# Pooled attention into soft mixture-of-experts slots, on one core: a first load in two parts, fewer and larger whole-row stores, fewer weight loads

## The chip, the core and the metric

The kernel runs on one core of a Trainium2 chip. The metric is the time of one execution on the device in microseconds (us). Engines are named as in the profile: PE is TensorE (its weight loads are PEld), DVE VectorE, ACT ScalarE, POOL GpSimd, SP SyncE. Transfers between memory and the on-chip buffers run on 16 DMA engines. Two queues feed them here: POOL issues the software transfers (q0 in the profile), which can turn float32 into bfloat16 on the way, and SP issues the hardware transfers (q1). SPq and POOLq mean the sequencers of these engines.

## The reference

```python
def attn(q, k, v):                       # each [8, 8, 576, 64] float32
    k_p = k.reshape(B, H, 72, 8, D).mean(axis=3)      # keys pooled by 8
    v_p = v.reshape(B, H, 72, 8, D).mean(axis=3)
    scores = (1 / sqrt(D)) * (q @ k_p.transpose(0, 1, 3, 2))
    return softmax(scores) @ v_p
def moe(x, phi, w1, w2):                 # x [4608, 512], phi [512, 32]
    logits = x @ phi                     # 8 experts x 4 slots
    slot_input = softmax(logits, over tokens).T @ x
    for e in range(8):                   # w1[e] [512, 1024], w2[e] [1024, 512]
        slot_out[e] = relu(slot_input[e] @ w1[e]) @ w2[e]
    return softmax(logits, over slots) @ slot_out      # [4608, 512] float32
```

The inputs are 28.3 MB of q, k and v and 33.6 MB of w1 and w2, all float32; the output is 9.4 MB.

## The kernel before, in words

**Attention.** The batch is worked off in four pairs (`NP`), two batch rows each. For each pair, `prepare_kq` pools the keys by matrix products with `pmat` (`pool_stage`), turns them and turns the queries; `prepare_v` does the same for the values and folds phi in by `iphi`. `score_unit` makes the scores and their exponentials, `u_tile` the weighted sums, `combine` (with `dispatch` and `turn`) adds the pair to the slot sums `G` and writes the transposed exponentials to `cT`.

**Loads.** Four buffers `big[:, 0..3]` hold k, q and v of the pairs in turn. `load` puts one of them in the POOL queue as a software transfer of 128 partitions by 4608 elements. The hooks `after_k`, `after_q` and `after_v` are called where a buffer has been read for the last time, and issue the next loads: first those of the next pair, then w1 (`load_w1`, into `w1_sb`), then w2 (`load_w2`, into the buffers that are free by then: `big`, `qTa`, `xsa`). The last expert and half of the one before come in eight pieces (`PIECES` times two halves of the columns, L446). POOL works in its written order. A software transfer signals one of eight semaphores in turn, so its issue can also wait for the landing of the transfer eight places ahead of it.

The very first load is different: the first 4 x 8 x 64 keys of each partition (128 rows of 8 KB, 1 MB) come by the SP queue as float32 into `kf` (L121), and DVE and ACT turn them to bfloat16 (L154, L155). The rest of these keys is the first transfer of the POOL queue (L122).

**Experts.** After the last pair, `hidden(0)` and `hidden(1)` multiply the slot inputs by w1 (four experts each), `turn_hidden` transposes, and `second_layer` multiplies by w2, expert by expert, into `so_ps`. The engines PE, ACT, DVE and SP work in the written order from here. The last expert's columns are done in two halves, so that `begin(0)` and `tiles` can scale and store the left half of the first ten output tiles while w2 for the right half is still coming.

**Output.** The 36 output tiles of 128 tokens by 512 columns are gathered in groups. A group of `rows` tiles covers 128 x `rows` consecutive tokens; partition p holds `rows` consecutive output rows, so a store of the whole group writes `rows` x 2 KB in one run for each partition. `tokens(n)` picks the columns of `cT` for a tile with a step of rows/2. The first four groups (2, 2, 2 and 4 tiles) are stored in halves of the columns. The others are stored whole, as soon as the group's last tile has been scaled by DVE or ACT (`put`, alternating), by one SP transfer each (`store`, L545).

Of the kernel before, what the change touches and what calls it, by code (L numbers as in the profile page):

```python
# [18 lines left out]
def kernel(  # L19
# [10 lines left out]
    nc = tc.nc  # L30
# [11 lines left out]
    NP = B // 2  # L42
# [11 lines left out]


    GROUPS, base = [], 0
    for rows in (2, 2, 2, 4, 4, 6, 10, 6):
        GROUPS.append((rows, base))
        base += 128 * rows
    TILES = [(g, r) for g, (rows, _) in enumerate(GROUPS) for r in range(rows)]  # L60
# [8 lines left out]
    big = persist.tile([128, 4, KQ], BF)  # L69
# [15 lines left out]
    def pair_of(src, pair):  # L85
        return src[2 * pair:2 * pair + 2].rearrange("b h (i t) d -> (b h i) (t d)", t=NT)
# [10 lines left out]
    def load(src, pair):  # L97
        nonlocal loaded
        loaded += 1
        t = big[:, loaded % 4]  # L100
        nc.gpsimd.dma_start(out=t, in_=pair_of(src, pair))
        return t.rearrange("p (t d) -> p t d", d=D)

    def load_w1(e, n, parts=((0, 128),)):
        for p0, p1 in parts:
            nc.gpsimd.dma_start(out=w1_sb[p0:p1, e:e + n].rearrange("p e j f -> p e (j f)"),
                                in_=moe_w1[e:e + n].rearrange("e (p j) f -> p e (j f)", j=DJ)[p0:p1])
# [3 lines left out]
    def load_w2(home, e, n, j0=0, j1=FJ):  # L111
        for i in range(n):
            for j in range(j0, j1):
                w2_at[e + i, j] = home[:, i, j * DM:(j + 1) * DM]
        nc.gpsimd.dma_start(out=home[:, 0:n, j0 * DM:j1 * DM],
                            in_=moe_w2[e:e + n].rearrange("e (p j) d -> p e j d", j=FJ)[:, :, j0:j1].rearrange("p e j d -> p e (j d)"))


    CUT = 4 * POOL * D
    kf = exf[:, 0:CUT]  # L120
    nc.sync.dma_start(out=kf, in_=pair_of(k, 0)[:, 0:CUT])  # L121
    nc.gpsimd.dma_start(out=big[:, 0, CUT:KQ], in_=pair_of(k, 0)[:, CUT:KQ])  # L122
    q_sb, k_sb, v_sb = {}, {}, {}
    k_sb[0] = big[:, 0].rearrange("p (t d) -> p t d", d=D)
# [37 lines left out]
    with tc.tile_pool(name="tmp", bufs=1) as tmp:  # L162
# [8 lines left out]
        for r in range(2):  # L171
            rows = slice(r * D, (r + 1) * D)
            nc.vector.tensor_copy(out=iphi[rows, :, 0:D],
                                  in_=ident[rows, rows].rearrange("p d -> p () d").to_broadcast([D, H, D]))
# [25 lines left out]
    def after_k(p):  # L200
        if p + 1 < NP:
            q_sb[p + 1] = load(q, p + 1)
        if p == 1:
            load_w1(0, 1, ((0, 112), (112, 120), (120, 128)))
        if p == NP - 1:
            load_w2(big[:, 0:2], 0, 2)

    def after_q(p):
        if p + 1 < NP:
            v_sb[p + 1] = load(v, p + 1)  # L210
        if p == 1:
            load_w1(1, 1)
        if p == 2:
            load_w1(2, 2)
            load_w1(4, 2)
            load_w1(6, 2)

    def after_v(p):
        if p + 2 < NP:
            k_sb[p + 2] = load(k, p + 2)  # L220
        if p == NP - 1:
            load_w2(big[:, 2:4], 2, 2)

    PARTS = ((0, 4), (4, NR))

# [23 lines left out]
    def prepare_kq(pair):  # L249

        means = kvpool.tile([128, NR, 2, D], BF, name="kmeans")
        yield from pool_stage(k_sb[pair], means, lambda: after_k(pair))
        kp[pair] = kvpool.tile([128, BH, SP], BF, name="kp", bufs=2)
        yield from turn_stage(means, kp[pair])
        for n, t0 in enumerate(range(0, NU, 6)):
            ps = ps_m.tile([128, 6, BH, NI], BF, name="q_ps", tag="m")
            for t in range(6):
                tt = 2 * (t0 + t)
                nc.tensor.transpose(out=ps[:, t].rearrange("p n i -> p (n i)"),  # L259
                                    in_=q_sb[pair][:, tt:tt + 2, :].rearrange("p t d -> p (t d)"), identity=ident)  # L260
            dst = qT[pair][:, :, t0:t0 + 6, :].rearrange("p n t i -> p t n i")
            if n % 3 == 1:
                nc.scalar.copy(out=dst, in_=ps)  # L263
            else:
                nc.vector.tensor_copy(out=dst, in_=ps)  # L265
            if n == NU // 6 - 1:
                after_q(pair)
            yield

    def prepare_v(pair):  # L270

        means = kvpool.tile([128, NR, 1, D], BF, name="vmeans")
        yield from pool_stage(v_sb[pair], means, lambda: after_v(pair))
        vpar = kvpool.tile([D, BH, SP], BF, name="vpar")
        yield from turn_stage(means, vpar)
        for b in range(2):
            for qd in range(2):
                ps = ps_m.tile([SP, HQ, XW], FP, name="v_ps", tag="m")
                for hh in range(HQ):
                    h = qd * HQ + hh  # L280
                    nc.tensor.matmul(out=ps[:, hh], lhsT=vpar[:, b * H + h], rhs=iphi[0:D, h], start=True, stop=True)
                nc.scalar.copy(out=vp[(2 * pair + b) % 5][:, qd * HQ:(qd + 1) * HQ, 0:XW], in_=ps)
                yield
# [158 lines left out]
    for half, cols in enumerate(halves):  # L442
        for e, j0, j1 in PIECES:
# [3 lines left out]
                                in_=moe_w2[e].rearrange("(p j) d -> p j d", j=FJ)[:, j0:j1, cols])  # L447
# [188 lines left out]
```

## Time and profile before

| | |
|---|---|
| median of 3 runs | 176.18 us (175.78 to 176.47) |
| the profiled execution, its own time | 175.6 us |
| its span, first to last instruction | 173.8 us |
| PE, DVE, ACT busy | 74%, 52%, 48% of the span |
| software queue q0 | 7072 packets, 30.48 MB written, 86.4% of 16 engines |
| hardware queue q1 | 3456 packets, 10.49 MB, 15.4% |
| HBM read, written | 61.93 MB, 9.44 MB |

The profile covers one execution. Its span is cut into 40 slices of 4.35 us, for which the page gives each engine's busy share in tenths and the DMA engines' share and rate. The rate counts the bytes as they are written: a load that turns float32 into bfloat16 reads twice the bytes it is counted with. So about 216 GB/s of such loads and about 435 GB/s of float32 loads or stores are the same load on the read side or the write side of the DMA engines.

### The profile page before, as it was taken

Reading aid. Unit: us, or ns where it says so; the run is one execution under the profiler, and the core shown is the slowest. Engines: PE = TensorE matmul, PEld = TensorE weight load, DVE = VectorE, ACT = ScalarE, POOL = GpSimd, SP = SyncE. Lnnn points to the kernel's source line nnn. Section 1 sums busy time; section 2 is a strip of 40 time slices with the busy share of each in tenths; the row PEclk is TensorE's granted clock in tenths of the full one; section 3 lists DMA queues with packets and bytes.
Section 4 is the critical chain, followed back from the end, with each engine's and each line's share of the span. In section 5 each row is a group of like instructions: output and inputs, shape, how many; then the busy total and the mean of one; then the engine's idle time right before and its main releaser. Section 6 shows DMA issues by size and latency. Waiting matters only on the chain.

```text
span 173.8 us, 3094 instructions
## 1 busy us (share of the span) xinstructions
PE 129.4 (74%) x1239; PEld 76.9 (44%) x1240; DVE 90.9 (52%) x251; ACT 83.0 (48%) x155; POOL 20.3 (12%) x38
## 2 busy tenths in 40 slices
PE   5205889999999998979998897889973096798000
PEld 2003555766677665756765455534451032332000
DVE  4403242487777879758798668614260002599100
ACT  3200248976767469755698941450120004799000
POOL 7000111132110060100100004041010030000000
PEclk9955799999999999999999995555599569999755
DMA  5999999999999999999999999999999999999995
GB/s 190 246 221 219 218 218 209 218 216 214 218 212 207 216 216 216 214 221 215 215 213 213 215 222 217 217 213 211 217 219 221 202 193 197 308 359 409 437 437 226
DMA packets 10542, 41.14 MB, mean 237 GB/s; under 512 B 785, under 2 KB 6417, under 8 KB 6689
## 3 DMA queue, kind: packets, MB, share of 16 engines
q0 software_dynamic: 7072, 30.48, 86.4%
q1 hardware_dynamic: 3456, 10.49, 15.4%
q8 instruction: 9, 0.15, 0.3%
q14 instruction: 5, 0.03, 0.0%
HBM read 61.93 MB, written 9.44 MB: 411 GB/s over the span
## 4 chain that ended last, share of the span: by engine, by line
DMA 46%; PE 26%; issue 7%; DVE 5%; ACT 5%; POOL 2%; DVEq 0%; POOLq 0%; ACTq 0%
DMA qTa<-in_moe_w_dram 20%; DMA big<-in_q_dram 14%; DMA phi_f<-in_moe_phi_dram 7%; PE pool_ps L231 6%; DMA xsa<-in_moe_w_dram 6%; PE sc L290 5%; PE u_ps L304 4%; DVE w_sb L529 4%; PE q_ps L259 4%; ACT exa L292 3%; PE G_ps L326 2%; PE lg_ps L322 1%; PE turn_ps L244 1%; PE f_ps L554 1%; ACT qTa L263 1%
## 5 line engine op out<-in xcount | busy, mean ns | idle before, releaser
L292 ACT ACTIVATE exa<-sc 72x576 bf16<-72x576 f32 x64 | 39.1, 649 | 11.7 <-PE sc L290 11.3
L315 DVE TENSOR_TENSOR xsa<-u_ps,rec 128x384 bf16<-128x384 f32 x69 | 37.7, 552 | 1.4
L304 PE MATMUL u_ps<-vp,exa 72*128 72x97 bf16 (+1 forms) x320 | 27.1, 221 | 1.4 <-DVE xsa L315 1.3
L290 PE MATMUL sc<-qTa,kp 64*72 64x288 bf16 x128 | 23.2, 304 | 1.8 <-ACT exa L292 1.7
L304 PEld LDWEIGHTS <-exa 72*128 72x128 bf16 (+1 forms) x320 | 17.7, 106 | 10.7 <-DVE xsa L315 3.6
L231 PE MATMUL pool_ps<-big,pmat 128*128 128x320 bf16 (+1 forms) x128 | 20.2, 303 | 0.5 <-DMA big<-in_k_dram 0.5
L309 DVE RECIPROCAL rec<-u_ps 128x4 f32<-128x4 f32 x72 | 12.4, 176 | 15.1 <-PE u_ps L304 14.6
L231 PEld LDWEIGHTS <-pmat 128*128 128x128 bf16 x128 | 12.4, 103 | 5.0 <-DMA big<-in_k_dram 0.6
L259 PE MATMUL q_ps<-ident,big 128*128 128x128 bf16 x144 | 11.7, 219 | 2.3 <-DMA big<-in_q_dram 1.2
L554 PE MATMUL f_ps<-so,cT 128*128 128x512 bf16 (+1 forms) x42 | 10.2, 337 | 1.8 <-ACT w_sb L527 0.8
L290 PEld LDWEIGHTS <-kp 64*72 64x72 bf16 x128 | 8.5, 107 | 6.7 <-issue 2.3
L326 PE MATMUL G_ps<-xsa,ee 128*128 128x512 bf16 x36 | 10.7, 441 | 0.8 <-ACT ee L323 0.7
L259 PEld LDWEIGHTS <-big 128*128 128x128 bf16 x144 | 8.6, 97 | 5.1 <-issue 1.8
L265 DVE COPY qTa<-q_ps 128x768 bf16<-128x768 bf16 x16 | 8.9, 555 | 3.8 <-PE q_ps L259 3.6
L529 DVE TENSOR_SCALAR w_sb<-f_ps,recR 128x512 f32<-128x512 f32 (+1 forms) x17 | 10.5, 683 | 0.2
L529 DVE TENSOR_SCALAR so<-so_ps,recC 128x256 bf16<-128x256 f32 x2 | 1.0, 484 | 18.0 <-PE so_ps L496 18.0
L527 ACT ACTIVATE w_sb<-f_ps,recR 128x512 f32<-128x512 f32 (+1 forms) x17 | 9.6, 638 | 0.4 <-PE f_ps L554 0.2
L263 ACT COPY qTa<-q_ps 128x768 bf16<-128x768 bf16 x8 | 6.3, 793 | 6.3 <-PE q_ps L259 6.3
L446 POOL DMA_DIRECT2D xsa<-in_moe_w_dram x8 | 5.6, 706 | 31.2 <-DVE recR L365 9.2
L182 PE MATMUL phi_ps<-spread,sel 128*128 128x256 bf16 x4 | 1.4, 384 | 9.5 <-DVE spread L177 9.5
L527 ACT ACTIVATE so_a<-so_ps,recC 128x256 bf16<-128x256 f32 x2 | 0.9, 474 | 14.9 <-PE so_ps L496 14.8
L496 PEld LDWEIGHTS <-hT 128*32 128x32 bf16 x76 | 2.3, 102 | 12.2 <-issue 11.3
(90 smaller groups left out, 152.7 us busy)
## 6 DMA issues: line engine op xcount, KB each, us to landing
w_sb<-in_moe_w_dram POOLq DMA_DIRECT2D x3, 2048.0 KB, 37.6
big<-in_q_dram POOLq DMA_DIRECT2D x4, 1152.0 KB, 13.1
big<-in_v_dram POOLq DMA_DIRECT2D x4, 1152.0 KB, 16.9
big<-in_moe_w_dram POOLq DMA_DIRECT2D x2, 2048.0 KB, 44.9
big<-in_k_dram POOLq DMA_DIRECT2D x3, 1152.0 KB, 21.4
out_dram<-w_sb SPq DMA_DIRECT2D x2, 1536.0 KB, 8.7
out_dram<-w_sb SPq DMA_DIRECT2D x1, 2560.0 KB, 9.2
qTa<-in_moe_w_dram POOLq DMA_DIRECT2D x1, 2048.0 KB, 34.5
```

The costliest lines, as they stand in the source:

```text
L231: nc.tensor.matmul(out=ps, lhsT=pmat, rhs=src[:, r0 * POOL + t:r1 * POOL:POOL, :], start=(t == 0), stop=(t == POOL - 1))
L259: nc.tensor.transpose(out=ps[:, t].rearrange("p n i -> p (n i)"), in_=q_sb[pair][:, tt:tt + 2, :].rearrange("p t d -> p (t d)"), identity= ...
L265: nc.vector.tensor_copy(out=dst, in_=ps)
L290: nc.tensor.matmul(out=ps[:, r, 0:S // 2], lhsT=kp[pair][rows, n], rhs=qT[pair][rows, n].rearrange("p t i -> p (t i)"), start=True, stop=True)
L292: nc.scalar.activation(out=dst.rearrange("p r (i t) -> p r i t", t=NU), in_=ps[:, :, 0:S // 2].rearrange("p r (t i) -> p r i t", i=NI), fu ...
L304: nc.tensor.matmul(out=ps[rows, hh], lhsT=ex[b][:, hh].rearrange("p r t -> p (r t)")[:, c:c + rows.stop - rows.start], rhs=vp[(2 * pair + ...
L309: nc.vector.reciprocal(out=rec, in_=ps[:, :, XW])
L315: nc.vector.tensor_tensor(out=dst, in0=ps[:, :, 0:XW], in1=rec.rearrange("p h -> p h ()").to_broadcast([128, HQ, XW]), op=ALU.mult)
L326: nc.tensor.matmul(out=ps, lhsT=ee[:, t].rearrange("p g s -> p (g s)"), rhs=x[:, t, :, 0:D], start=(t == 0), stop=(t == 8))
L527: nc.scalar.activation(out=dst, in_=src, func=AF.Copy, scale=by)
L529: nc.vector.tensor_scalar(out=dst, in0=src, scalar1=by, scalar2=None, op0=ALU.mult)
L554: nc.tensor.matmul(out=ps, lhsT=tokens(n), rhs=so[:, cols], start=True, stop=True)
```

## The change

Three places are changed. The first keys come in two SP transfers, partitions 0 to 15 and then 16 to 127. The output groups after the first ten tiles have 6, 8 and 12 tiles where they had 4, 6, 10 and 6, so that there are three whole stores for four. Experts 2 to 7 of w1 come in two transfers of three experts where there were three of two; experts 0 to 3 of w2 come in one transfer of four, issued in `after_v` of the last pair, where there were two of two, the first of them issued in `after_k` of that pair.

```diff
-    for rows in (2, 2, 2, 4, 4, 6, 10, 6):
+    for rows in (2, 2, 2, 4, 6, 8, 12):
...
-    nc.sync.dma_start(out=kf, in_=pair_of(k, 0)[:, 0:CUT])
+    for p0, p1 in ((0, 16), (16, 128)):
+        nc.sync.dma_start(out=kf[p0:p1], in_=pair_of(k, 0)[p0:p1, 0:CUT])
...
     def after_k(p):
...
-        if p == NP - 1:
-            load_w2(big[:, 0:2], 0, 2)
     def after_q(p):
...
         if p == 2:
-            load_w1(2, 2)
-            load_w1(4, 2)
-            load_w1(6, 2)
+            load_w1(2, 3)
+            load_w1(5, 3)
     def after_v(p):
...
         if p == NP - 1:
-            load_w2(big[:, 2:4], 2, 2)
+            load_w2(big, 0, 4)
```

The order of the instructions on PE, DVE and ACT stays as it was. On POOL two transfers are gone; on SP one load is added ahead and one store is gone at the end.

## The prediction

> **What bounds the kernel now.** I read the 40 slices of the page first, then the DMA shares of chosen stretches, then the order of issues on POOL and SP. From the page:
>
> ```profile
> DMA  5999999999999999999999999999999999999995
> GB/s 190 246 221 219 218 218 209 218 216 214 218 212 207 216 216 216 214 221 215 215 213 213 215 222 217 217 213 211 217 219 221 202 193 197 308 359 409 437 437 226
> ```
>
> The 16 DMA engines are nine tenths busy or more in every slice but the first and the last. No arithmetic engine comes near that. Until about 147 us the rate is that of loads that turn float32 into bfloat16 (some 216 GB/s written, twice that read), and from then on that of the stores. The kernel is one long stream of transfers, and an edit changes the time only as far as it changes when the stream starts, how many bytes per us it moves, whether it ever runs dry, or when the last byte leaves. The stretches (us, PE, PEld, DVE, ACT, POOL busy, clock, DMA share, GB/s) show the head, and the even run behind it:
>
> ```profile
> 0.74:1.75 1.01, 0.00 (x0) 0.00 (x0) 0.73 (x1) 1.01 (x1) 0.51 (x1) 1.00 0.00 0
> 1.75:2.25 0.50, 0.26 (x1) 0.13 (x2) 0.50 (x9) 0.47 (x2) 0.50 (x2) 1.00 1.15 213
> 2.25:2.75 0.50, 0.50 (x2) 0.15 (x1) 0.44 (x2) 0.00 (x0) 0.43 (x2) 1.00 0.73 229
> 2.75:3.25 0.50, 0.50 (x3) 0.15 (x2) 0.31 (x2) 0.00 (x0) 0.49 (x2) 1.00 0.97 344
> 3.25:4.00 0.75, 0.75 (x3) 0.30 (x2) 0.00 (x0) 0.00 (x0) 0.75 (x2) 1.00 0.88 371
> 4.00:4.75 0.75, 0.75 (x3) 0.30 (x2) 0.00 (x0) 0.00 (x0) 0.63 (x2) 1.00 1.07 433
> 9.50:14.00 4.50, 0.00 (x0) 0.00 (x0) 0.00 (x0) 0.00 (x0) 0.00 (x0) 0.50 1.01 216
> 50.00:51.00 1.00, 1.00 (x16) 0.77 (x15) 0.63 (x2) 0.69 (x1) 0.53 (x1) 1.00 1.06 217
> 51.00:52.00 1.00, 1.00 (x15) 0.62 (x14) 1.00 (x5) 0.38 (x1) 0.00 (x0) 1.00 1.11 218
> 52.00:53.00 1.00, 1.00 (x11) 0.66 (x10) 0.85 (x3) 0.42 (x2) 0.00 (x0) 1.00 1.00 175
> 53.00:56.00 3.00, 3.00 (x37) 2.12 (x35) 2.20 (x7) 2.62 (x5) 0.00 (x0) 1.00 1.01 211
> 80.00:120.00 40.00, 35.90 (x340) 21.34 (x338) 27.02 (x80) 21.96 (x46) 5.28 (x8) 0.81 1.03 216
> ```
>
> And the tail:
>
> ```profile
> 155.00:156.00 1.00, 0.80 (x4) 0.35 (x3) 1.00 (x2) 1.00 (x3) 0.00 (x0) 1.00 1.06 376
> 156.00:157.00 1.00, 1.00 (x4) 0.35 (x3) 1.00 (x3) 1.00 (x3) 0.00 (x0) 1.00 1.06 444
> 157.00:158.50 1.50, 1.30 (x6) 0.56 (x5) 1.50 (x3) 1.40 (x3) 0.00 (x0) 1.00 0.99 404
> 158.50:162.00 3.50, 1.80 (x7) 0.41 (x4) 3.07 (x5) 2.24 (x4) 0.00 (x0) 1.00 1.05 442
> 162.00:168.00 6.00, 0.00 (x0) 0.00 (x0) 0.00 (x0) 0.00 (x0) 0.00 (x0) 0.56 1.02 437
> 168.00:172.20 4.20, 0.00 (x0) 0.00 (x0) 0.00 (x0) 0.00 (x0) 0.00 (x0) 0.50 0.89 375
> 172.20:173.80 1.60, 0.00 (x0) 0.00 (x0) 0.00 (x0) 0.00 (x0) 0.00 (x0) 0.50 0.00 0
> ```
>
> The first byte moves at 1.75 us and the last at 172.2; 1.6 us of closing follow. Every engine that computes is idle from 162 on, so the last 10 us are the stores alone.
>
> I count against the profiled execution, 175.6 us with a span of 173.8, so 1.8 us lie outside the span. The median of the runs shown is 176.18, 0.6 higher; a difference found in the profile is carried over to the median unchanged. Half a percent is 0.88 us, about what a measurement of this kernel can tell from no change; the three runs shown lie 0.7 us apart.
>
> **The head: 16 rows, then 112.** The load is issued once on SP:
>
> ```profile
> 0.74 0.38 SPq L121 DMA_DIRECT2D exa<-in_k_dram  x1
> ...
> DVE spread L177 <- DMA phi_f<-in_moe_phi_dram: 6.6, 1, 6.6
> ```
>
> It holds SP for 0.38 us, and its first byte moves 1.01 us after the issue begins. Then the rate climbs slowly. Against 433 GB/s the four stretches from 1.75 to 4.00 miss 220 x 0.5 + 204 x 0.5 + 89 x 0.5 + 62 x 0.75 = 303 KB, which is 0.70 us of the stream. The change adds one issue on SP, ahead of nothing but the second part of the same load: SP's next transfer is an output. It may gain in two ways. A load of 16 descriptors may be ready sooner than one of 128 (at most the 0.38 us that the issue takes), and the slow first accesses may overlap with the second issue (at most 0.70). It may lose in two ways: the second transfer may be late on engines that have finished their one row, or a transfer to 16 partitions may not run at the full rate. 16 rows are an eighth of the 1024 KB, 131 KB, 0.30 us at 433 GB/s. The second issue ends 0.38 us behind the first, so a hole between them should be under 0.1 us. For a narrow transfer the nearest rows are 50 to 53 us, where w1's first expert comes in 112, 8 and 8 rows: 217, 218 and 175 GB/s, then 211. The dip costs (211 - 175) / 211 x 1 us = 0.17 us for two narrow transfers, if it is theirs at all. I take 0.2 gained by an earlier start (half of the 0.38) and 0.2 lost by the narrow rows, so 0.0; the ends are -0.9 (an earlier start and half of the slow ramp) and +1.2.
>
> The rule that speaks against this edit stands in the Trainium skill, SBUF — State Buffer, section Door 1: partitions 0 to 15 reach four of the 16 ports, for which the page measures 104 GB/s. An estimate by that page is 131 KB / 104 GB/s = 1.26 us, 0.96 more than the 0.30, and with it the sum below would be about 177.1 for 176.1. The two 8-row loads of the trace do not show a loss of that size, but those rows wait for reads twice as large as the writes, and other transfers were in the queue to fill in.
>
> What waits for the first keys is DVE and ACT's copy, and behind it on DVE the rows up to `spread` (L177), which then stand 6.6 us for phi. So a landing later by a microsecond or two costs the arithmetic nothing. Only the stream's place counts.
>
> **w1 and w2 in two transfers less.** POOL's issues, and when a w1 load lands (DMA to landing, us, least, median, most, for the seven loads into `w_sb`):
>
> ```profile
> DMA to landing us min/median/max: 17.8/21.6/46.6
> ...
> 61.45 2.16 POOL L106 DMA_DIRECT2D w_sb<-in_moe_w_dram  x3
> 72.24 0.71 POOL L115 DMA_DIRECT2D big<-in_moe_w_dram  x1 [8.63 <-PE u_ps L304]
> 86.07 0.70 POOL L115 DMA_DIRECT2D big<-in_moe_w_dram  x1 [13.12 <-PE pool_ps L231]
> ...
> 129.45 0.74 POOL L446 DMA_DIRECT2D xsa<-in_moe_w_dram  x1 [9.24 <-DVE recR L365]
> 139.17 0.74 POOL L446 DMA_DIRECT2D xsa<-in_moe_w_dram  x1 [8.98 <-DMA qTa<-in_moe_w_dram]
> 141.64 0.59 POOL L446 DMA_DIRECT2D xsa<-in_moe_w_dram  x1 [1.73 <-DMA xsa<-in_moe_w_dram]
> ```
>
> The bytes and the runs per partition stay. Two issues of about 0.7 us on POOL go, but they are hidden: the last of the three w1 loads is issued before 63.6 us and lands 46.6 us later, so some 45 us of work stand in the queue. Experts 0 and 1 of w2 are now issued at 86.07 for 72.24, and the queue has work until about 63 + 46.6 = 109 us; the cover is 23 us. If it were gone, each late issue would leave the engines idle for its lateness. Between transfers the stream has no gap that can be seen: 80 to 120 us, with several boundaries, runs at 216 GB/s, as does 9.5 to 14 inside few. One part in 216 of a 9.7 us load (2.1 MB at 216 GB/s) is 0.05, so two boundaries less bring at most 0.1; I take -0.05.
>
> The Trainium skill, DMA: Bandwidth & Descriptors, section Anatomy of one DMA, gives about 2.0 us of fixed cost for each transfer. If that stood in the stream, the change as a whole (two software loads and a store less, one load more) would bring 4 us, 172.2. The even 216 GB/s speaks against it: here that cost is latency under a full queue.
>
> Two waits move. The last two pieces are issued when `qTa` and the first part of `xsa` have landed (139.17, 141.64), because they share semaphores with them. With two transfers less, the piece eight places behind is still the third and fourth of the right half, so these stay. The piece at 129.45 waited for the second w2 load and now waits for the joined one, which lands at the same byte of the stream. On PE, `second_layer` starts later than that landing and then waits for `qTa`:
>
> ```profile
> 129.88 1.91 PE L496 MATMUL so_ps<-big,hT 128*32 128x512 bf16 x32
> 138.66 1.90 PE L496 MATMUL so_ps<-qTa,hT 128*32 128x512 bf16 x16 [6.87 <-DMA qTa<-in_moe_w_dram]
> ```
>
> All 32 products of the four experts run together from 129.88, so no one used experts 0 and 1 earlier, and 6.9 us of idle follow. Cost 0.
>
> **Groups of 6, 8 and 12.** The whole stores are issued when their last tile is scaled:
>
> ```profile
> 154.40 0.34 SPq L545 DMA_DIRECT2D out_dram<-w_sb  x1
> ...
> 156.38 0.34 SPq L545 DMA_DIRECT2D out_dram<-w_sb  x1
> ...
> 159.67 0.33 SPq L545 DMA_DIRECT2D out_dram<-w_sb  x1
> ...
> 161.65 0.33 SPq L545 DMA_DIRECT2D out_dram<-w_sb  x1
> ```
>
> These are the ends of tiles 13, 19, 29 and 35, and (161.65 - 154.40) / 22 = 0.33 us per tile. The new ends are tile 15 at 155.06, tile 23 at 157.7 and tile 35 at 161.65. The rate of the stores rises from 376 to 444 GB/s at about 155.9, where the first whole store takes over from the half-width ones. A tile is 262 KB, 0.60 us at 438 GB/s. Before, the store issued at 154.40 had 1.5 us of lead over its turn. Now the first of six tiles has 0.8 us, against 1.01 us from issue to first byte at the head, so the engines may stand for 0.2 us; on an idle engine the latency may also be less. I take +0.1. Six tiles last 3.6 us, to 159.6, and the store of eight is issued at 157.7; eight last 4.8, to 164.4, and the store of twelve is issued at 161.65. Both are in time, by 0.9 and 1.7 us over the latency. The end itself doesn't depend on the size of the last store, as it is queued long before its turn. A boundary between stores may cost something: 157 to 158.5, which holds one, runs at 404 against 442, 0.13 us. One boundary less is worth 0 to 0.13; I take -0.1. Ten tiles in one store are not faster than six (437 and 442), so larger rows bring nothing.
>
> **Sum.** 0.0 - 0.05 + 0.1 - 0.1 = -0.05 us. That is 175.55 for such an execution, and 176.1 for the median.
>
> **The rivals.** (1) Slower: the two head transfers are served one after another, or the 16 rows crawl. The second then repeats a part of the ramp (0.70) or the start (1.01), or the 16 rows run at a quarter of 433 GB/s and take 1.21 for 0.30 us. Price about +1.1, 177.2; it decides from a loss of about 0.9 us on the engines that end last. For it: the rate at the head is already far under 433, so there is something there that is paid per start. Against it: the second issue follows within 0.4 us, and the dip at 52 us is small. The Trainium skill, DMA: Bandwidth & Descriptors, section Rules for kernel authors, says of two transfers to disjoint partition halves "Don't bother — they serialize"; no run here shows it yet. (2) Faster: the slow ramp comes from 128 descriptors made at once, and 16 pass at once. Then up to 0.70 and the 0.2 of the earlier start go, with -0.05: 175.2. For it: the share is 0.73 at 2.25 to 2.75 us although a whole load is queued. (3) Much faster, by a fixed cost per transfer in the stream, 172.2; the even rate is against it. That the change does nothing of what it says I leave out: the two loads on SP and the joined ones on POOL stand in its order of instructions.
>
> **How the numbers follow.** Forecast, within 0.5%: 0.64. Rival 1: 0.20, all slower. Rival 2 and 3: 0.14 and 0.02, faster. The range is 175.2 to 177.3: it goes down to rival 2 and up to just past rival 1, and leaves out the dearer half of each.
>
> **What would show it.** Right: first bytes by 1.75 us or sooner, SP's second issue by 1.2, the rate at 433 GB/s by about 4 us, the software loads beginning at 4.8 as now; an unbroken 216 GB/s from 80 to 138; the first whole store issued at about 155.1 and the share of the DMA engines at 155.5 to 156.5 not under 0.9; the last byte at about 172.1. Wrong: a stretch under 200 GB/s after 2.25 us, the first keys landing later than 6 us, a DMA share under 0.8 at 156, or POOL issuing its last pieces later than 143.

## The result, and the profile after

The changed kernel takes 176.68 us (median of 20 runs, 176.24 to 178.41) against 176.22 us (median of 20) before. The ratio is 1.0036, with a 95% interval of 1.0019 to 1.0053: 0.63 us slower, or 0.3 to 0.9. I had forecast no change. The time lies in the range and within the half percent of the likeliest case, but it moved, and to the side that I gave one chance in five.

The profiled execution took 176.29 us, with a span of 174.5 (175.6 and 173.8 before). Its slices, from the page after:

```profile
DMA  6999999999999999999999999999999999999994
GB/s 167 237 215 224 213 220 215 215 215 219 212 212 219 211 217 217 220 210 217 218 216 214 216 218 214 216 216 220 214 218 216 205 193 194 301 349 436 451 451 180
```

It is still one stream of transfers, nine tenths busy from the second slice to the last but one. What moved is at the two ends: 167 for 190 GB/s in the first slice, 451 for 437 among the whole stores. The head by stretches, after (us, busy times by engine, clock, DMA share, GB/s):

```profile
0.74:1.75 1.01, 0.00 (x0) 0.00 (x0) 0.73 (x1) 1.01 (x1) 0.50 (x1) 1.00 0.00 0
1.75:2.25 0.50, 0.26 (x1) 0.13 (x2) 0.50 (x9) 0.47 (x2) 0.50 (x2) 1.00 1.12 295
2.25:2.75 0.50, 0.50 (x2) 0.15 (x1) 0.45 (x2) 0.00 (x0) 0.44 (x2) 1.00 1.32 197
2.75:3.25 0.50, 0.50 (x3) 0.15 (x2) 0.31 (x2) 0.00 (x0) 0.49 (x2) 1.00 0.46 164
3.25:4.00 0.75, 0.75 (x3) 0.30 (x2) 0.00 (x0) 0.00 (x0) 0.75 (x2) 1.00 1.08 360
4.00:4.75 0.75, 0.75 (x3) 0.30 (x2) 0.00 (x0) 0.00 (x0) 0.63 (x2) 1.00 1.08 350
```

A packet is counted here with all its bytes and all its time in the stretch in which it begins, so a share can be over 1 and the stretch behind it low. The rate divided by the share, the rate for a full share, says how fast the packets went.

Three things are to be seen. The first byte still moves at 1.75 us: 16 rows start no sooner than 128. The first packets are shorter than before (295 / 1.12 = 263 GB/s for a full share, before 213 / 1.15 = 185), so the 16 rows don't crawl. But those that begin from 2.25 to 2.75, where the first packets of the second transfer are due, are long (197 / 1.32 = 149, before 229 / 0.73 = 314). And at 4.00 to 4.75 the rate doesn't reach 433 but 350, at the same DMA share (1.08 for 1.07). The engines are as busy as before, so each packet takes them longer: 350 / 1.08 = 324 GB/s for a full share, where before there were 433 / 1.07 = 405.

The packets of the hardware queue from 1 to 11 us are those of the first keys (packets, MB, share of 16 engines). Before, and then after:

```profile
q1 hardware_dynamic: 144, 1.05, 30.0%
...
q1 hardware_dynamic: 160, 1.05, 38.0%
```

So the same megabyte takes 3.0 us of each engine before and 3.8 us after. The issues of software loads, before (KB each, median us from issue to landing), show what becomes of it:

```profile
big<-in_k_dram POOLq DMA_DIRECT2D x1, 640.0 KB, 7.6
phi_f<-in_moe_phi_dram POOLq DMA_DIRECT2D x1, 64.0 KB, 11.5
```

And after:

```profile
big<-in_k_dram POOLq DMA_DIRECT2D x1, 640.0 KB, 8.3
phi_f<-in_moe_phi_dram POOLq DMA_DIRECT2D x1, 64.0 KB, 12.2
```

Both land 0.7 us later, phi with all of the first queries ahead of it. Nothing gives that back: from 80 to 120 us the rate is 216 GB/s as before, the first store is issued at 147.12 us where it was 146.45, and the span is 0.7 us longer. At the tail, after (SP's issue, then two stretches):

```profile
155.69 0.34 SPq L543 DMA_DIRECT2D out_dram<-w_sb  x1
...
155.50:156.50 1.00, 0.80 (x4) 0.23 (x3) 1.00 (x3) 1.00 (x3) 0.00 (x0) 1.00 0.97 346
156.50:157.50 1.00, 1.00 (x5) 0.48 (x4) 1.00 (x2) 1.00 (x3) 0.00 (x0) 1.00 1.08 447
```

The first whole store, now of six tiles, is issued 0.9 us ahead of its first packet (156.61 us), and the share stays at 0.97: no hole.

Of the signs that I had named for being wrong, the first keys landed at 6.9 us (before 5.9), later than 6. A stretch under 200 GB/s after 2.25 us came too, but it says little: two kernels with one first load have such a stretch (164 in the kernel before run again, 180 in the changed kernel with one first load), since packets are counted where they begin.

### The profile page after: what moved, and what is told of

It is laid out like the page before. It is cut to its first block, busy times and chain, and to the rows that moved or that the text cites. A ratio compares the mean times of both kernels' runs of the same rounds, so it can differ in the third digit from the quotient of the medians.

```text
span 174.5 us, 3092 instructions
## 1 busy us (share of the span) xinstructions
PE 130.5 (75%) x1240; PEld 77.1 (44%) x1240; DVE 90.8 (52%) x251; ACT 83.1 (48%) x155; POOL 19.0 (11%) x36
## 4 chain that ended last, share of the span: by engine, by line
DMA 45%; PE 20%; issue 17%; DVE 5%; ACT 3%; POOL 2%; DVEq 0%; POOLq 0%; ACTq 0%
DMA qTa<-in_moe_w_dram 19%; DMA big<-in_q_dram 14%; DMA phi_f<-in_moe_phi_dram 7%; PE pool_ps L229 6%; DMA xsa<-in_moe_w_dram 6%; DVE w_sb L527 4%; PE q_ps L257 4%; PE sc L288 3%; PE u_ps L302 2%; PE G_ps L324 1%; ACT exa L290 1%; PE f_ps L552 1%; PE turn_ps L242 1%; ACT qTa L261 1%; POOL big L101 1%
## 5 line engine op out<-in xcount | busy, mean ns | idle before, releaser
L290 ACT ACTIVATE exa<-sc 72x576 bf16<-72x576 f32 x64 | 39.1, 650 | 13.0 <-PE sc L288 12.6
L307 DVE RECIPROCAL rec<-u_ps 128x4 f32<-128x4 f32 x72 | 12.4, 176 | 14.4 <-PE u_ps L302 14.0
L229 PEld LDWEIGHTS <-pmat 128*128 128x128 bf16 x128 | 12.3, 103 | 4.7 <-issue 0.4
L257 PE MATMUL q_ps<-ident,big 128*128 128x128 bf16 x144 | 11.7, 219 | 2.3 <-DMA big<-in_q_dram 1.2
L324 PE MATMUL G_ps<-xsa,ee 128*128 128x512 bf16 x36 | 12.0, 484 | 0.8 <-ACT ee L321 0.7
L444 POOL DMA_DIRECT2D xsa<-in_moe_w_dram x8 | 5.6, 704 | 30.3 <-DVE hT L486 11.6
L494 PEld LDWEIGHTS <-hT 128*32 128x32 bf16 x76 | 2.3, 102 | 11.7 <-issue 10.8
## 6 DMA issues: line engine op xcount, KB each, us to landing
big<-in_moe_w_dram POOLq DMA_DIRECT2D x1, 4096.0 KB, 42.9
```

What stands on the lines that cost most here:

```text
L229: nc.tensor.matmul(out=ps, lhsT=pmat, rhs=src[:, r0 * POOL + t:r1 * POOL:POOL, :], start=(t == 0), stop=(t == POOL - 1))
L290: nc.scalar.activation(out=dst.rearrange("p r (i t) -> p r i t", t=NU), in_=ps[:, :, 0:S // 2].rearrange("p r (t i) -> p r i t", i=NI), fu ...
L307: nc.vector.reciprocal(out=rec, in_=ps[:, :, XW])
L324: nc.tensor.matmul(out=ps, lhsT=ee[:, t].rearrange("p g s -> p (g s)"), rhs=x[:, t, :, 0:D], start=(t == 0), stop=(t == 8))
```

## The experiments

All ratios are against the kernel before on the same chip in the same hour, with their 95% intervals. Different experiments ran on different chips.

**How far equal kernels come apart.** Half of the differences here are under half a percent, so the kernel before was run against itself.

> The kernel before, unchanged, as a kernel of its own: how far two equal kernels come apart. If differences of a few tenths of a percent belong to the single build and load, its ratio lies as far from 1.000 as those of 0.3 to 0.6% that have been seen; if not, it is within 0.1% of 1.000.

Ratio 1.0001 (0.9980 to 1.0022). An interval reaches 0.2% to each side; differences below that are not told apart here. In its trace phi lands 11.8 us after its issue, for 11.5 in the first trace of the same kernel.

**The head alone.**

```diff
-    nc.sync.dma_start(out=kf, in_=pair_of(k, 0)[:, 0:CUT])
+    for p0, p1 in ((0, 16), (16, 128)):
+        nc.sync.dma_start(out=kf[p0:p1], in_=pair_of(k, 0)[p0:p1, 0:CUT])
```

> The kernel before, with the first keys in 16 rows and then 112 and nothing else changed. Theory H (the whole loss is made at the head): the first packets of the software queue come 0.6 us later than before, as in the changed kernel, and the time is 0.6 to 0.7 us over the kernel before (ratio 1.0035 to 1.004). Theory T (the loss comes from the groups or the joined weight loads): within 0.1 us of before.

Ratio 1.0063 (1.0034 to 1.0091), 1.1 us and at least 0.6. Its head:

```profile
2.75:3.25 0.50, 0.50 (x3) 0.15 (x2) 0.31 (x2) 0.00 (x0) 0.50 (x2) 1.00 0.45 131
3.25:4.00 0.75, 0.75 (x3) 0.29 (x2) 0.00 (x0) 0.00 (x0) 0.75 (x2) 1.00 1.05 339
4.00:4.75 0.75, 0.75 (x3) 0.29 (x2) 0.00 (x0) 0.00 (x0) 0.62 (x2) 1.00 0.99 328
...
phi_f<-in_moe_phi_dram POOLq DMA_DIRECT2D x1, 64.0 KB, 12.3
```

The same dip and the same slow packets. The first software packet begins 0.9 us later than before (5.65 us for 4.74; 5.38 in the changed kernel), and phi lands 0.8 us later. The head by itself makes the whole loss.

**Everything but the head.** The changed kernel with the first keys in one transfer again.

> The changed kernel with the first keys in one transfer again; groups of 6, 8 and 12 and the joined w1 and w2 loads stay. Theory H: 0.1 to 0.15 us under the kernel before (ratio about 0.999), with the whole stores taking 15.97 us for 16.05. Theory T: 0.5 us or more over it.

Ratio 1.0005 (0.9983 to 1.0028), phi 11.6 us after its issue. The loss goes with the split. The small gain that I expected of the rest is below what can be told.

**Two transfers that both cover all partitions.** The same bytes in the first transfer as 16 rows have, but taken from all 128:

```diff
+    for c0, c1 in ((0, CUT // 8), (CUT // 8, CUT)):
+        nc.sync.dma_start(out=kf[:, c0:c1], in_=pair_of(k, 0)[:, c0:c1])
```

> The kernel before, with the first keys in two transfers of all 128 partitions each: the first eighth of the columns (1 KB per partition) and then the rest (7 KB). As many bytes in the first transfer as 16 rows have. Theory A (a transfer loses when its rows don't cover the 128 partitions, since then several DMA engines write to the same rows' part of the buffer): the rate reaches 430 GB/s by 4 us as before, and the time is within 0.15 us of before. Theory B (every further transfer at the head pays its start again): 0.5 to 0.7 us over before, like the 16 and 112 rows.

Ratio 1.0040 (1.0019 to 1.0061).

```profile
2.75:3.25 0.50, 0.50 (x3) 0.16 (x2) 0.31 (x2) 0.00 (x0) 0.49 (x2) 1.00 0.83 215
3.25:4.00 0.75, 0.75 (x3) 0.30 (x2) 0.00 (x0) 0.00 (x0) 0.75 (x2) 1.00 0.99 344
4.00:4.75 0.75, 0.75 (x3) 0.30 (x2) 0.00 (x0) 0.00 (x0) 0.63 (x2) 1.00 0.85 354
...
phi_f<-in_moe_phi_dram POOLq DMA_DIRECT2D x1, 64.0 KB, 11.9
```

Here neither theory is right alone. The packets run at full speed again (354 / 0.85 = 416 GB/s for a full share), but the slow stretch up to 3.25 us is there (215 GB/s, before 344), and phi lands at 11.9, just behind the 11.5 and 11.8 of the kernel before. So a second start costs something. That the rows cost more shows in the packets and not in the ratio, which is no lower than that of the changed kernel.

**Halves of the rows against halves of the columns.** The same bytes per transfer, cut in the one way or the other: `(0, 64), (64, 128)` for the rows, `(0, CUT // 2), (CUT // 2, CUT)` for the columns.

> The kernel before, with the first keys in two transfers of 64 rows. Theory A: each half covers half of the partitions and runs at about half of 433 GB/s, so 1 MB takes up to 4.8 us for 2.4: 1.5 to 2.4 us over before. Theory B: 0.5 to 0.7 us over before, as for any split in two.

> The kernel before, with the first keys in two transfers of all 128 partitions and half of the columns each (4 KB per partition), to be held against two transfers of 64 rows, which have the same bytes and lost 2.2 us. Theory A plus a small price for any second transfer: the second load of the software queue lands 0.2 to 0.3 us later than before, as with an eighth of the columns, and the rate at 3.25 to 4.75 per unit of DMA share is that of before. Theory B (the price is the second start alone): as late as with 64 rows, 1.6 us.

Rows: ratio 1.0144 (1.0108 to 1.0179). Columns: 1.0062 (1.0038 to 1.0086) from four runs. First the halves of the rows (SP's two issues, then a stretch of the head):

```profile
0.74 1.23 SPq L122 DMA_DIRECT2D exa<-in_k_dram  x2
...
3.25:4.00 0.75, 0.75 (x3) 0.30 (x2) 0.00 (x0) 0.00 (x0) 0.75 (x2) 1.00 1.15 273
...
phi_f<-in_moe_phi_dram POOLq DMA_DIRECT2D x1, 64.0 KB, 13.3
```

Then the halves of the columns:

```profile
3.25:4.00 0.75, 0.75 (x3) 0.29 (x2) 0.00 (x0) 0.00 (x0) 0.75 (x2) 1.00 0.97 388
4.00:4.75 0.75, 0.75 (x3) 0.29 (x2) 0.16 (x1) 0.00 (x0) 0.63 (x2) 1.00 1.00 410
...
phi_f<-in_moe_phi_dram POOLq DMA_DIRECT2D x1, 64.0 KB, 11.5
```

The packets of a half of the rows run at 273 / 1.15 = 237 GB/s for a full share, those of a half of the columns at 388 / 0.97 = 400 and 410. (Later stretches can't be used for the rows: from 4.17 us on the software queue's packets, which write at about 216, run between theirs.) That is theory A, if not quite half. A smaller part of the loss is another: SP takes 1.23 us for these two issues, where 16 and 112 rows take it 0.85, and the first packet begins at 2.13 us and not at 1.75. In its trace the column split lets phi land at 11.5 as before, while its four runs said 0.6%.

> Two transfers of all 128 partitions and half the columns each, once more and with more runs. Its trace had the software loads only 0.1 us later than before, its four runs 0.6% over. If the trace has the whole cost: ratio 1.000 to 1.002. If a second start costs more than the trace of one run shows: 1.004 to 1.008 again.

Ratio 1.0018 (0.9999 to 1.0036) from twelve runs, phi at 11.7. This is the same kernel on another chip, and the two intervals don't meet: between chips a ratio can come out some 0.4% apart, more than an interval says. By the three ratios of this kind (1.0040, 1.0062, 1.0018) a second start with all partitions costs 0.3 to 1.1 us; more closely it isn't settled by time.

**112 rows first.** The last question at the head: is it the 16 rows that clog the stream, or do the 112 run slowly themselves?

```diff
-    for p0, p1 in ((0, 16), (16, 128)):
+    for p0, p1 in ((0, 112), (112, 128)):
```

> The kernel before, with the first keys in 112 rows and then 16: the same two sizes in the other order. Theory A (rows that don't cover the 128 partitions in the usual way make every packet longer): the 112 rows run slowly from the start, some 330 to 350 GB/s at 3.25 to 4.75 us for 371 and 433 before, and the time is 0.6 to 1.1 us over before. Theory N (the 16 rows at the front are what clogs the stream): 433 GB/s by 4 us, and the loss falls to 0.3 us or less, or moves to the first software loads at 5 to 7 us.

Ratio 1.0089 (1.0066 to 1.0111).

```profile
3.25:4.00 0.75, 0.75 (x3) 0.30 (x2) 0.00 (x0) 0.00 (x0) 0.75 (x2) 1.00 1.09 328
4.00:4.75 0.75, 0.75 (x3) 0.30 (x2) 0.00 (x0) 0.00 (x0) 0.63 (x2) 1.00 0.99 306
...
phi_f<-in_moe_phi_dram POOLq DMA_DIRECT2D x1, 64.0 KB, 12.6
```

With nothing narrow ahead of them, 112 rows run at 328 / 1.09 = 301 and 306 / 0.99 = 309 GB/s for a full share. So the larger part is slow by itself, and the loss of 1.6 us is more than the 0.6 to 1.1 that theory A expected.

**All heads side by side.** The share of 1 to 11 us that the first keys' packets take of the 16 engines, as a time for each engine, is the closest measure that the traces give:

| first keys in | time per engine, us | phi, us | ratio |
|---|---|---|---|
| one transfer (seven traces) | 2.90 to 3.14 | 11.5 to 12.4 | |
| two, all partitions, an eighth of the columns first | 3.33 | 11.9 | 1.0040 |
| two, all partitions, half the columns each (two runs) | 3.31, 3.20 | 11.5, 11.7 | 1.0062, 1.0018 |
| 16 rows, then 112 (alone; in the changed kernel) | 3.85, 3.80 | 12.3, 12.2 | 1.0063, 1.0036 |
| 112 rows, then 16 | 3.88 | 12.6 | 1.0089 |
| 64 rows, then 64 | 4.38 | 13.3 | 1.0144 |

So of the 0.8 us per engine that 16 and 112 rows add, 0.2 to 0.3 comes with any second start and the rest with rows that don't cover the 128 partitions. Why such packets are slower is not shown: a cut by rows changes what is read as well as where it is written. Phi alone can mislead. The 12.4 belongs to a kernel with one first load (the last one below, with expert 0 of w1 in one transfer as well). There one of the 16 engines landed the rest of the keys late, at 9.65 us for 8.87 before, while the first engine landed them at 8.1 as before.

**The groups alone and the loads alone.**

> The kernel before with groups of 6, 8 and 12 alone. By the traces of the changed kernels the stretch from the first store to the last byte is 0.12 us shorter: ratio 0.999 to 1.0. If the first whole store, now of six tiles, leaves the DMA engines idle: 0.1 us or more slower, with a DMA share under 0.9 at 155.5 to 156.5.

> The kernel before with the joined w1 and w2 loads alone. If boundaries between transfers cost next to nothing and the later issue is hidden: ratio 1.000, within 0.1%. If two boundaries cost as much as a transfer's fixed price: 2 us and more faster. If the joined loads make the slowest engine land later: 0.1 to 0.3% slower, with the stores beginning later and 24.9 us from the first store to the last byte as before.

Groups: 0.9984 (0.9962 to 1.0006). Loads: 0.9982 (0.9962 to 1.0003). Both lean to the faster side and neither is clear of 1. By the packets of the traces, the time from the first byte stored to the last was 24.87 us before (24.87 again in its second trace, 24.88 with the head split alone, 24.84 with the loads alone; 24.83 to 24.90 in all kernels with the old groups but one) and 24.76, 24.75 and 24.81 us in the three kernels that have the new groups and the joined loads. In the trace of groups alone it was 25.1, for another reason:

```profile
148.00:149.00 1.00, 0.86 (x10) 0.44 (x13) 0.79 (x2) 0.77 (x3) 0.00 (x0) 1.00 0.55 150
149.00:150.00 1.00, 0.71 (x14) 0.30 (x13) 0.87 (x3) 0.82 (x3) 0.00 (x0) 1.00 0.43 132
```

In that execution (176.97 us, the slowest of twelve; the fastest took 175.47) the first store was issued at 147.58 us, and the DMA engines stood half idle at 148 to 150. The last weight load had landed on 15 of the engines by 148.83 us and on the last one at 150.24. What the arithmetic waits for at the end is the slowest of the 16. The gain of the groups alone is therefore not shown by their own trace.

**The narrow loads in the middle.** In the prediction I had used w1's first expert, 112, 8 and 8 rows, as a witness. It was put into one transfer of 128 rows, `load_w1(0, 1)`, in the kernel before, and in the changed one with its first keys in one transfer.

> The kernel before, with expert 0 of w1 in one transfer of 128 rows for 112, 8 and 8. Behind these narrow loads every trace so far has a dip (175 GB/s at 52 to 53 us before, 138 and 166 in the kernel with one first load). Theory A, extended to software loads: the dip goes, 0.2 to 0.5 us, ratio 0.997 to 0.999. Rival: the dip has another cause, and nothing changes (1.000) or the spread of the 16 engines grows and the time with it.

> The changed kernel with the first keys in one transfer and expert 0 of w1 in one transfer; groups of 6, 8 and 12 and the joined loads stay. If the tail gains 0.12 us as the trace of the changed kernel says and the dip goes too: 0.3 to 0.6 us under before, ratio 0.9965 to 0.998. If only the tail gains: 0.999.

Ratios 1.0033 (1.0016 to 1.0050) and 1.0024 (1.0011 to 1.0037): slower, both. The stretch behind these loads:

```profile
52.00:53.00 1.00, 1.00 (x12) 0.66 (x10) 0.85 (x4) 0.47 (x1) 0.00 (x0) 1.00 0.92 194
```

That is 194 for 175 GB/s, but the traces that keep the narrow loads have 138 (before again) and 194 (loads alone) in the same stretch, so the dip isn't shown to be theirs. By its packets the last weight load ended 0.4 us later on the slowest engine (149.18 us for 148.80), and 0.1 us earlier on the mean of the 16. That fits a loss of balance between the engines; it is one trace, and the cause stays open. Both expectations were wrong: no gain came. Whether the change really costs 0.2 to 0.3% is less sure. Both kernels ran on the chip where half the columns lost 0.6%, and that loss was 0.4% smaller on another chip.

## Why the prediction was wrong

**What bounds the kernel** held: one stream of transfers, and what is lost at its head comes out at its end, 0.67 us later at the first store and 0.7 in the span.

**The head** is the step that failed. I had set 0.2 us gained by an earlier start against 0.2 lost by narrow rows. The earlier start isn't there: first byte at 1.75 us with 16 rows as with 128. The term that I put at 0.0 measured +0.7 us: so much later come the software loads and the first store, and the first keys' packets take 3.8 us of each engine for 3.0. The loss isn't made by the 16 rows, whose own packets were quick (263 GB/s for a full share). I had priced a narrow transfer and not its complement; 112 rows move at 301 to 333 GB/s for a full share where 128 reach 405 to 422. A smaller part, 0.2 to 0.3 of the 0.8 us, is paid for the second start. I had named that start in rival 1 with +1.1 us and a chance of 0.20. It was the right kind of mechanism, at 0.6 of its price in the whole change, and it took in the rows only as the 16. The share of 0.73 that I read for rival 2 stands right behind one of 1.15 and is an effect of where packets are counted.

**The witness** was the wrong one. The 8-row loads of w1 lie in a full queue, read twice what they write, and their removal doesn't bring the dip's 0.17 us. They could not stand for a narrow load with nothing beside it. And the dip was not shown to be theirs: that stretch has 138, 175 and 194 GB/s in three traces with the same loads. The page that I had quoted against the change (the Trainium skill, SBUF — State Buffer, section Door 1) gave a sum of about 177.1 for 176.1, on the right side. But the loss didn't come where that sum puts it. Its figure for 16 partitions, 104 GB/s, isn't what this trace shows: of their 16 packets (131 KB), 14 had ended by 2.47 us, 0.7 us after the first began, where the sum has 1.26 us. Its figure for 64 partitions, 196 GB/s, is under the 237 of the halves and points the same way. The rule of the Trainium skill against splitting over partitions (DMA: Bandwidth & Descriptors, section Rules for kernel authors) also holds: every split of the rows lost, 0.4 to 1.4%. That page of the Trainium skill, section The descriptor swizzle, tells how in a 128-partition transfer each engine writes one port; that 112 rows lose by leaving this order fits the longer packets, and no run shows the ports themselves.

**The joined loads** were rightly priced at about nothing (forecast -0.05; 0.9982, within its interval of 1). The sum of 172.2 by a fixed 2.0 us per transfer is excluded. POOL's issues and PE's wait, after:

```profile
86.44 0.76 POOL L115 DMA_DIRECT2D big<-in_moe_w_dram  x1 [22.75 <-PE pool_ps L229]
...
115.48 2.79 POOL L444 DMA_DIRECT2D xsa<-in_moe_w_dram  x4 [7.68 <-PE G_ps L324]
129.87 0.74 POOL L444 DMA_DIRECT2D xsa<-in_moe_w_dram  x1 [11.60 <-DVE hT L486]
139.82 0.74 POOL L444 DMA_DIRECT2D xsa<-in_moe_w_dram  x1 [9.21 <-DMA qTa<-in_moe_w_dram]
142.33 0.59 POOL L444 DMA_DIRECT2D xsa<-in_moe_w_dram  x1 [1.78 <-DMA xsa<-in_moe_w_dram]
...
139.30 1.90 PE L494 MATMUL so_ps<-qTa,hT 128*32 128x512 bf16 x16 [6.49 <-DMA qTa<-in_moe_w_dram]
```

The last pieces wait for the same two landings, and PE still stands 6.5 us for `qTa`. The piece at 129.87 comes half a microsecond after the joined load's landing (86.44 + 42.9 us), which fits the forecast, though the profile names DVE for the wait. One wait that I hadn't listed is gone: before, the fourth piece stood 3.2 us for the first w2 load and was issued at 119.47; now it is one of the four at 115.48. Under a full queue that brought nothing that can be seen.

**The groups.** One boundary less was put at -0.1. Three traces lean that way (24.75 to 24.81 us of stores for 24.83 to 24.90), the trace of the groups alone doesn't, and their ratio can't tell it from nothing: the term stays open. The hole before the six-tile store, +0.1, didn't come: 0.9 us from issue to its first packet was enough.

With 0.7 for the head's 0.0 and 0 for the hole's 0.1, the sum would have been about +0.55 us; the ratio says 0.63. That they agree so closely is partly luck, as the head alone measured 1.1 us, and at least 0.6.

## What to carry to other kernels

In a kernel that is one queue of transfers, look at the first microseconds as at a stage of its own: a slow start is paid in full at the end, however far away the end is. A transfer that must be cut should be cut along the free dimension (halves: 0.2 to 0.6% lost, against 1.4% by rows), and both pieces of a cut by rows must be priced, the large one too. A witness from the middle of a full queue says little about a transfer that runs alone.

## What the runs showed of the hardware

With 8 KB per row, the packets of a transfer of 64 of the 128 rows run at 237 GB/s for a full share, those of 112 at 301 to 333, those of 128 at 405 to 422. The first byte comes about 1.0 us after SP's issue begins when 16, 112 or 128 rows are asked for, and 1.4 us after it with 64, whose issue takes SP 0.6 us for 0.4. And an execution's time depends on the slowest of the 16 DMA engines: in the trace of the groups alone, one that landed its last weights 1.4 us behind the next left the engines half idle for 2 us at the end.
